# Reordering ten rows of the output projection by column tile, and five weight chunks in place of six, in a one-token attention and MLP kernel

## The chip, the cores and the metric

The kernel runs on one core of one Trainium2 chip. The metric is the device time of one execution in microseconds (us). A ratio is the mean time of one kernel's fast runs over that of the kernel before in the same rounds on the same chip, so it is not quite the ratio of the medians quoted beside it. Verdicts are given at 2%. The profile's span runs from the first to the last instruction and is some 1.3 to 1.7 us shorter than the time.

## The reference, cut to what matters

One token goes through a layer norm, then through attention (32 heads, 4 key/value heads, the last 4096 positions of the cache) and an MLP, and both are added to it:

```python
def reference(A_x, A_k_cache, A_v_cache, A_wq, A_wo, B_x, B_w1, B_b1, B_w2, B_b2):
    # ... q = x @ wq, softmax over 4096 keys, o = p @ v ...
    # attention ends in  o.reshape(B, Sq, Hq * Dh) @ wo      (4096 x 1024)
    # MLP:  h = gelu(y @ w1 + b1);  h @ w2 + b2              (1024 x 3584, 3584 x 1024)
    x = A_x
    xn = _layernorm(x, axis=-1)
    return x + _A_ref(xn, ...) + _B_ref(xn, ...)
```

With one token, every weight is read once and used for one row. About 40 MB have to come in (39.88 MB in the profile), and there is little arithmetic. The last weight in the stream is wo, which TensorE takes as 32 rows of 128 x 1024, each as two matmuls of 512 columns, one for each half of the output.

## The kernel before

All large transfers go through one queue, in program order. wo comes last, in chunks, each with a semaphore of its own:

```python
W2_CHUNKS = [28]
WO_CHUNKS = [15, 9, 4, 2, 1, 1]
WO_IN_W1 = sum(WO_CHUNKS[:2])
# ... the two halves of the output lie in PSUM on partitions 0 and 32: here called two column tiles
    ACC = [PS[32 * n: 32 * n + 1, (6 + n) * 512: (7 + n) * 512] for n in range(2)]
# ...
    for j, nj in enumerate(WO_CHUNKS):
        if j0 == WO_IN_W1:
            sp.wait_ge(PE.sem, pe_sc)
        sp.dma_start(wo_at(j0, nj), wo_pm[:, j0 * D:(j0 + nj) * D]).then_inc(s_wo[j], 16)
        j0 += nj
# ...
    for j, nj in enumerate(WO_CHUNKS[:-1]):
        pe.wait_ge(s_wo[j], 16)
        for _ in range(nj):
            for n in range(2):
                pe.matmul(ACC[n], lhsT=OP[:, r:r + 1], rhs=wo_at(r, 1)[:, n * 512:(n + 1) * 512],
                          start=False, stop=False)
            r += 1
# ... the last row stands in a block of its own, followed by the casts and the output
    with nc.body("pe_last", valid_engines=TENSOR):
        pe.wait_ge(s_wo[-1], 16)
        # ... two matmuls ...
        last.then_inc(s_fin, 1)
```

Just before this loop, 56 matmuls of the same kind work off w2 (L537), and before those 32 matmuls take the values of the attention (L504). "Column tile" means no more here than what the trace of this kernel shows: the two matmuls of a wo or w2 row, into partitions 0 and 32, start 3 to 7 ns apart, while the 32 of L504, all into partitions 0 to 31, start 0.216 us apart at full clock and 0.427 at half.

## Time and profile before

| | before |
|---|---|
| time, median of the first 3 runs | 98.81 us (98.73 to 98.90) |
| span of the profiled run | 97.6 us |
| bytes moved, mean rate | 39.88 MB, 409 GB/s |
| TensorE busy | 67.3 us (69%) |
| mean granted clock | 0.895 |

These are lines of the page's second part: the span in 40 equal slices of 2.44 us, with the busy tenths of TensorE, the granted clock in tenths of full speed, and the busy tenths of the transfers.

```profile
PE   0001299959992039988999982169994799891991
PEclk9999999999999655999999999955699759999579
DMA  7999999989999989979999998889994999899970
```

The transfers are busy almost everywhere. TensorE has holes, and a few slices after some of them the clock dips to half. The last dip lies in the tail, a few slices from the end. The other views (chain, timeline, windows) are shown in the prediction.

### The profile page before, as it was taken

The page shows a single profiled execution, that of the slowest core. Times are in us where ns is not written, and L with a number is a line of the kernel's source. Part 1 is how long each engine was busy: PE and PEld are TensorE (multiplying, and loading weights), DVE is VectorE, ACT ScalarE, POOL GpSimd, SP SyncE. Part 2 cuts the span into 40 slices and gives each one's busy share as a digit, 9 for nine tenths or more (in the row PEclk, how much of TensorE's full clock was granted, in tenths as well). Part 3 has the DMA queues.
Part 4 walks back from the last instruction along what each step waited for, and adds up shares of the span by engine and source line. Part 5 has one row for each costly group of instructions (what it writes and reads, how often), then busy time and mean ns, then how long its engine had stood idle before and what let it go on. Part 6 is the DMA issues. An engine that isn't in the chain of part 4 may idle for free.

```text
span 97.6 us, 1050 instructions
## 1 busy us (share of the span) xinstructions
PE 67.3 (69%) x330; PEld 31.8 (33%) x330; DVE 36.0 (37%) x49; ACT 5.8 (6%) x11; POOL 7.1 (7%) x23
## 2 busy tenths in 40 slices
PE   0001299959992039988999982169994799891991
PEld 0001255525541025645654421033341233330330
DVE  3705530000008999600999515794005300000002
ACT  0500060000001000000000000400000000000002
POOL 6795000000000000000000000000000000000000
PEclk9999999999999655999999999955699759999579
DMA  7999999989999989979999998889994999899970
GB/s 215 430 432 431 431 430 430 430 346 426 490 446 470 399 376 517 423 336 430 430 430 423 423 671 376 376 376 399 634 470 201 428 466 466 383 408 401 413 272 8
DMA packets 2773, 39.88 MB, mean 409 GB/s; under 512 B 322, under 2 KB 340, under 8 KB 724
## 3 DMA queue, kind: packets, MB, share of 16 engines
q1 hardware_dynamic: 2738, 39.85, 96.0%
q8 instruction: 1, 0.02, 0.1%
q10 hardware_dynamic: 34, 0.01, 0.1%
HBM read 39.86 MB, written 0.00 MB: 408 GB/s over the span
## 4 chain that ended last, share of the span: by engine, by line
DMA 82%; PE 13%; SPq 2%; issue 1%; DVE 1%; POOLq 0%
DMA W<-in_B_w_dram 42%; DMA W<-in_A_wo_dram 40%; PE PS L387 7%; PE PS L548 5%; SPq L168 1%; DVE KV L567 1%; SPq L178 0%; SPq L426 0%; SPq L162 0%; PE PS L557 0%; POOLq L260 0%
## 5 line engine op out<-in xcount | busy, mean ns | idle before, releaser
L344 DVE STREAM_TRANSPOSE KV<-KV 128x4096 bf16<-128x4096 bf16 x4 | 17.5, 4424 | 5.7 <-DMA KV<-in_A_k_cache_dram 5.7
L387 PE MATMUL PS<-W,YZ 128*97 x64 | 14.7, 387 | 4.6 <-POOLq L260 4.5
L335 PE MATMUL PS<-WA,PT 128*97 x64 | 15.5, 404 | 1.3 <-POOLq L260 1.2
L387 PEld LDWEIGHTS PS<-W,YZ 128*97 x64 | 8.7, 136 | 10.6 <-issue 7.8
L335 PEld LDWEIGHTS PS<-WA,PT 128*97 x64 | 8.5, 132 | 8.0 <-issue 3.7
L504 PE MATMUL PS<-KV,PT 128*32 128x512 bf16 x32 | 9.7, 479 | 0.1
L548 PE MATMUL PS<-W,OP 128*1 128x512 bf16 x48 | 7.2, 461 | 2.3 <-DMA W<-in_A_wo_dram 2.3
L537 PE MATMUL PS<-WA,GT 128*1 128x512 bf16 x56 | 7.9, 451 | 0.0
L567 DVE CAST KV<-PS 1x512 bf16<-1x512 f32 x1 | 0.7, 683 | 18.8 <-PE PS L557 18.8
L403 PE MATMUL PS<-KV,LQ 128*128 x32 | 7.1, 379 | 0.0
L295 PE MATMUL PS<-XT,meanf 128*128 128x16 f32 x2 | 0.6, 384 | 9.4 <-DVE XT L291 9.4
L347 DVE STREAM_TRANSPOSE TT<-PS 128x1024 f32<-128x1024 f32 x1 | 1.2, 1250 | 15.5 <-PE PS L335 15.5
L504 PEld LDWEIGHTS PS<-KV,PT 128*32 128x32 bf16 x32 | 3.7, 117 | 5.7 <-issue 3.7
L548 PEld LDWEIGHTS PS<-W,OP 128*1 128x1 bf16 x48 | 2.2, 94 | 6.8 <-DMA W<-in_A_wo_dram 2.5
L403 PEld LDWEIGHTS PS<-KV,LQ 128*128 x32 | 3.1, 98 | 3.9 <-issue 0.6
L537 PEld LDWEIGHTS PS<-WA,GT 128*1 128x1 bf16 x56 | 2.7, 96 | 4.7 <-issue 2.3
L295 PEld LDWEIGHTS PS<-XT,meanf 128*128 128x128 f32 x2 | 0.5, 310 | 9.4 <-DVE XT L291 9.4
L509 DVE TENSOR_TENSOR TT<-PS,RM 32x512 f32<-32x512 f32 x1 | 0.7, 678 | 7.0 <-PE PS L504 7.0
L451 ACT ACTIVATE Pe<-PS,NMB 128x512 bf16<-128x512 f32 x2 | 1.3, 683 | 29.1 <-DVE NMB L448 29.1
L205 DVE MEMSET PS<- 128x3072 f32 x1 | 2.6, 2618 | 0.6 <-issue 0.6
L430 DVE TENSOR_REDUCE MXP<-PS 128x1 f32<-128x1024 f32 x1 | 1.2, 1225 | 3.0 <-PE PS L403 3.0
L569 ACT ACTIVATE KV<-PS 1x512 bf16<-1x512 f32 x1 | 0.6, 586 | 29.5 <-PE PS L557 29.5
(87 smaller groups left out, 31.5 us busy)
## 6 DMA issues: line engine op xcount, KB each, us to landing
WA<-in_A_wq_dram SPq DMA_DIRECT2D x2, 4096.0 KB, 16.6
W<-in_B_w_dram SPq DMA_DIRECT2D x2, 3584.0 KB, 37.2
WA<-in_B_w_dram SPq DMA_DIRECT2D x1, 7168.0 KB, 46.2
KV<-in_A_k_cache_dram SPq DMA_DIRECT2D x4, 1024.0 KB, 34.1
KV<-in_A_v_cache_dram SPq DMA_DIRECT2D x4, 1024.0 KB, 43.3
W<-in_A_wo_dram SPq DMA_DIRECT2D x1, 3840.0 KB, 33.5
W<-in_A_wo_dram SPq DMA_DIRECT2D x1, 2304.0 KB, 38.6
KV<-in_A_wo_dram SPq DMA_DIRECT2D x1, 1024.0 KB, 34.4
```

The source lines that it names most:

```text
L205: d_ps = DVE.mark(dve.memset(PS[:, 0:6 * 512], 0.0))
L335: last = pe.matmul(PS[0:97, n * 512:(n + 1) * 512], lhsT=shifted(XZ, s)[:, bass.ds(k, 1), :], rhs=wq_rows[:, bass.ds(k, 1), s * 1024 + n * ...
L344: dve.transpose(out=KT[:, g * W:(g + 1) * W], in_=KT[:, g * W:(g + 1) * W]).then_inc(r_k, 1)
L347: DVE.mark(dve.transpose(out=TT[:, :], in_=PS[:, 0:1024]))
L387: last = pe.matmul(PS[0:97, (2 + n) * 512:(2 + n) * 512 + HW], lhsT=shifted(YZ, s)[:, bass.ds(k, 1), :], rhs=w1_rows[:, bass.ds(k, 1), c: ...
L403: last = pe.matmul(PS[:, (4 + n) * 512:(5 + n) * 512], lhsT=q_blocks[:, bass.ds(g, 1), j, :], rhs=k_blocks[:, bass.ds(g, 1), n, :, j, :], ...
L430: d_mxp = DVE.mark(dve.tensor_reduce(out=MXP[:, 0:1], in_=PS[:, 4 * 512:6 * 512], axis=AX.X, op=ALU.max))
L451: a_exp = ACT.mark(act.activation(out=Pe[:, n * 512:(n + 1) * 512], in_=PS[:, (4 + n) * 512:(5 + n) * 512], func=ACTF.Exp, scale=SCALE, bi ...
L504: last = pe.matmul(PS[0:32, 0:512].rearrange("p (g d) -> p g d", g=HKV), lhsT=PT[:, b * 32:(b + 1) * 32], rhs=Vb[:, b, :, :], start=(b == ...
L537: pe.matmul(ACC[n], lhsT=GT[:, c:c + 1], rhs=W2[:, c * D + n * 512: c * D + (n + 1) * 512], start=False, stop=False)
L548: pe.matmul(ACC[n], lhsT=OP[:, r:r + 1], rhs=wo_at(r, 1)[:, n * 512:(n + 1) * 512], start=False, stop=False)
L567: d_out = DVE.mark(dve.tensor_copy(OUT[32:33, :], ACC[1]))
```

## The change

The intent is to close the hole that TensorE has while it waits for the second wo chunk, without adding an instruction. Matmuls of the two halves normally run side by side on two column tiles (a pair every 0.216 us at full clock in the profile before). If ten rows are issued as ten matmuls of one half and then ten of the other, they should not pair (those of L504, on one tile, take 0.216 us each), TensorE should stay busy longer, and the clock should not fall before the tail. The chunks after the second become 5, 2 and 1 rows.

```diff
-WO_CHUNKS = [15, 9, 4, 2, 1, 1]
+WO_ALONE = 10
+WO_CHUNKS = [15, 9, 5, 2, 1]
...
-        for _ in range(nj):
-            for n in range(2):
-                pe.matmul(ACC[n], lhsT=OP[:, r:r + 1], rhs=wo_at(r, 1)[:, n * 512:(n + 1) * 512],
-                          start=False, stop=False)
-            r += 1
+        alone = WO_ALONE if j == 0 else 0
+        order = [(u, n) for n in range(2) for u in range(alone)] + [(u, n) for u in range(alone, nj) for n in range(2)]
+        for u, n in order:
+            pe.matmul(ACC[n], lhsT=OP[:, r + u:r + u + 1], rhs=wo_at(r + u, 1)[:, n * 512:(n + 1) * 512],
+                      start=False, stop=False)
+        r += nj
```

## The prediction

The change needs only the step of matmuls on one column tile, and the trace gives it: 0.216 us at full clock for L504. That the stream could give no more than its 430 to 432 GB/s is not shown.

> **What bounds the kernel now.** I read the page's chain of waits first, then the chain in order of time for the last 13 us, then the timeline of TensorE there, then the windows cut where the granted clock changes, and last each transfer's issue and landing. The chain by line:
>
> ```profile
> DMA 82%; PE 13%; SPq 2%; issue 1%; DVE 1%; POOLq 0%
> ...
> 51.43 38.63 DMA W<-in_A_wo_dram
> 90.06 0.04 issue
> 90.10 5.30 PE PS L548 x32
> 95.41 0.24 PE PS L557 x2
> 95.64 0.02 issue
> 95.67 0.68 DVE KV L567
> ```
>
> The first line is the share of the span by engine; the rest are start, length and owner. The kernel streams weights through one queue (39.88 MB, mean 409 GB/s over the span, about 430 in most slices), and the chain is that stream until the second wo chunk lands at 90.06 us. From there to the end it is TensorE: 32 matmuls of L548, then the last two. The timeline shows why these take over 5 us (start, length, engine, line, count, idle before):
>
> ```profile
> 76.53 7.89 PE L537 MATMUL PS<-WA,GT 128*1 128x512 bf16 x56
> 84.70 3.40 PE L548 MATMUL PS<-W,OP 128*1 128x512 bf16 x30 [0.28 <-DMA W<-in_A_wo_dram]
> 90.10 3.78 PE L548 MATMUL PS<-W,OP 128*1 128x512 bf16 x18 [2.00 <-DMA W<-in_A_wo_dram]
> 93.66 1.74 PE L548 MATMUL PS<-KV,OP 128*1 128x512 bf16 x14
> 95.24 0.38 PE L557 MATMUL PS<-KV,OP 128*1 128x512 bf16 x2
> ```
>
> 30 matmuls of the first chunk take 3.40 us, then TensorE stands idle 2.00 us, then 18 matmuls of the same form take 3.78 us. The windows (stretch, length, TensorE busy, granted clock, DMA share, GB/s) give the reason:
>
> ```profile
> 73.31:76.72 3.41, 1.28 (x11) 1.00 0.67 288
> 76.72:80.14 3.42, 3.42 (x18) 0.50 1.00 431
> 80.14:83.55 3.41, 3.41 (x34) 1.00 1.00 432
> 83.55:86.97 3.42, 3.14 (x32) 1.00 0.98 420
> 86.97:90.38 3.41, 1.41 (x16) 1.00 0.97 414
> 90.38:93.79 3.41, 3.41 (x20) 0.50 0.98 400
> 93.79:97.21 3.42, 1.83 (x18) 1.00 0.21 76
> ```
>
> The clock changes on a grid of 3.41 us. A cell with 1.28 or 1.41 us of work (37 and 41%) is followed by one at half clock; a full cell brings the full clock back. Another cell, 18.70 to 22.11, with 2.26 us of work (66%) was not followed by a fall. So the 2.00 us hole before the second chunk makes the next 3.41 us run at half clock, and TensorE falls behind the stream exactly in the tail. The individual starts are 0.216 us apart by pairs at full clock (0.427 at half), as the first chunk's line also gives: (3.40 - 0.38) / 14 steps between 15 pairs. The two halves of a row start only 4 ns apart, since they lie on different column tiles.
>
> How late TensorE is at the very end matters most. The last transfer is issued at 59.46 and takes 35.5 us, so it lands at about 95.0:
>
> ```profile
> 59.46 0.43 SPq L426 DMA_DIRECT2D KV<-in_A_wo_dram  x1
> ...
> DMA to landing us min/median/max: 35.5/35.5/35.5
> ...
> 95.05 0.08 PEld L557 LDWEIGHTS PS<-KV,OP 128*1 128x1 bf16 x2 [0.15 <-DMA KV<-in_A_wo_dram]
> ```
>
> TensorE took up the last row's weights at 95.05, just after that landing, and its matmuls began at 95.24, one pair step (0.216) after the previous pair at 95.02. So TensorE had nearly caught up: it is late by 0.1 to 0.2 us, not by the 1.7 us that the half clock cost it in between.
>
> [...]
>
> **The change part by part.** First, the ten rows half by half. The matmul count stays at 64 for wo and the sums are the same up to their order. Ten matmuls in a row on one column tile can't pair, so they take a step of 0.216 us each, then ten on the other. The first of the second tile can start with the tenth of the first, and at the other seam likewise, so the first chunk has 10 + 9 + 5 = 24 steps instead of 15. It starts at 84.70 as before; its last start is 84.70 + 23 x 0.216 = 89.67 and its busy time ends at 89.67 + 0.38 = 90.05. Waste of 9 x 0.216 = 1.94 us, laid exactly into the 2.00 us hole; the second chunk lands at 90.06. L504 shows that a stream on one tile counts as work: after a full cell of it (66.48 to 69.90) the clock came back.
>
> What it buys: the cell 86.97 to 90.38 becomes about 97% busy, so no half clock from 90.38. The nine rows of the second chunk then take 9 x 0.216 = 1.94, from 90.10 to 92.04 (next possible start), where before the tenth row started at 93.66. That is 1.6 us earlier.
>
> Second, the chunks. 4 2 1 1 rows become 5 2 1: same bytes, one transfer fewer, and the last chunk is still one row. Before, the landings are 90.06, then issue plus landing time: 58.14 + 34.4 = 92.5, 93.8, 94.4 and 95.0, that is about 0.615 us a row (256 KB at some 425 GB/s) whatever the chunk size. So five rows land at 90.06 + 5 x 0.615 = 93.14, two more at 94.37, the last at 94.99. [...]
>
> Third, the new tail. TensorE idles from 92.04 (busy to about 92.2) to 93.18, works 5 x 0.216 to 94.26, idles to 94.41, does two rows to 94.84, waits for 94.99 and starts the last pair at about 95.10 (landing to first matmul was 0.13 us for chunk one, 0.04 for chunk two). Before: 95.24. **The end comes 0.14 us earlier**; casts and output stay the same. The cell 90.38 to 93.79 has 1.8 + 0.6 = 2.4 us of work, 71%, over the 66% that kept the clock, so no new half clock there. The sum: 1.6 us gained on TensorE in the middle, 1.5 of them hidden behind the stream. 98.81 - 0.14 = 98.67.
>
> **The rivals.**
> One: the gain at the end equals the gain in the middle (1.6 us, 97.2, 1.6% faster). For it speaks that the chain of waits charges 5.5 us to TensorE after 90.10. Against it: the last chunk's landing at 95.0 doesn't depend on TensorE (no buffer is waited for after 59.46), and nothing can end before it.
> Two: the free phase. If the grid lies otherwise in other executions, the kernel before is not always hit. A cell must hold most of the 2.00 us hole to fall; with cells of 3.41 us I estimate that in 40 to 70% of phases. Where it is not hit, the kernel before also ends at the landing, and the change gives 0.00. Where the half clock starts later than 90.38, the loss before can be some 0.4 us. The small range of the times before (98.73 to 98.90) leaves room for at most about 0.2 us of this. It would make 98.75.
> Three: the waste makes TensorE late. If the half clock falls into the first chunk (a hole before 84.57), eight of its steps take 0.427, and it ends some 1.7 us late, at 91.6; nine, five and two rows then end at 93.5, 94.6 and 95.0, still about at the last landing. If two such things meet, the kernel would be slower by up to 0.5 us: 99.2. Single-tile steps slower than 0.216 would act the same way; 0.2 us of slack at 90.06 and 1.1 at 93.14 absorb 0.05 a step.
> Four: fewer, larger transfers move the last landing itself. Between chunks of 4, 2 and 1 rows the rate hardly differs, so at most some hundredths of a us.
>
> **Range and chances.** The expected gain is 0.14 us in this phase and 0.05 to 0.3 over phases; I keep 98.68. The spread of one kernel is about 0.2 to 0.3 us, larger than the gain. Faster by over 2% needs 96.8, below the landing plus output, which is ruled out unless the stream itself quickens; slower by 2% needs 2 us of new loss, more than the whole hole. So nearly all is within 2%, and the range is 98.45 to 98.95.
>
> **What would show the steps right or wrong.** In the timeline, the first chunk's 30 matmuls should last about 5.35 us (24 steps) and the idle time before the second chunk fall under 0.1 us. The windows after 90 should show clock 1.00, and the second chunk's 18 matmuls about 2.1 us. Waits for wo should appear before chunk three (about 1.0 us), and small ones before four and five, and the chain should end on the transfer, with only the last two matmuls after it. The last landing should stay at 95.0 and the span be 97.4 to 97.5. I'm wrong if the last landing moves by over 0.2 us, if the clock still falls to 0.50 after 90 with a full first chunk (a stream on one tile with one column would then not count as work), or if many executions differ through the phase.

## The result

| | before | after |
|---|---|---|
| time, median of 6 runs | 98.86 us (98.72 to 99.03) | 98.98 us (98.82 to 99.01) |
| ratio | | 1.0008, 95% interval 0.9994 to 1.0022 |
| span of the profiled run | 97.6 us | 97.6 us |
| mean granted clock | 0.895 | 0.913 |

A second measurement in another session (the relabelled run a_again below, with the same instructions) gave 98.72 us against 98.78 for the kernel before, ratio 0.9986 (0.9964 to 1.0008). The two ratios lie on either side of 1. The change moves the time by less than these runs can tell.

The chain of the changed kernel, by engine and then its last pieces in order of time (start, length, owner):

```profile
DMA 70%; PE 25%; SPq 1%; issue 1%; DVE 1%; POOLq 0%
...
58.29 34.94 DMA KV<-in_A_wo_dram
93.23 0.04 issue
93.27 1.24 PE PS L551 x10
...
95.14 0.04 issue
95.18 0.40 PE PS L560 x2
```

The chain now stays with the transfers until the third chunk lands at 93.23, and the last two matmuls start 0.04 us after the last landing (95.14). Before, they started some 0.2 us after theirs. So the end does what the prediction said. But the landing itself is 0.12 us later than in the profile before, and the span is the same. The timeline of TensorE (start, length, line, count, idle before):

```profile
75.99 6.21 PE L538 MATMUL PS<-WA,GT 128*1 128x512 bf16 x56
84.86 8.30 PE L551 MATMUL PS<-W,OP 128*1 128x512 bf16 x48 [2.65 <-DMA W<-in_A_wo_dram]
93.27 1.86 PE L551 MATMUL PS<-KV,OP 128*1 128x512 bf16 x14
```

This is another history than in the profile before. The w2 matmuls took 6.21 us, not 7.89, and the hole lies in front of the first wo chunk, 2.65 us long, not in front of the second. The wait before chunk three, told as about 1.0 us, is 0.11 us (84.86 + 8.30 = 93.16 to 93.27). The windows, cut on the 3.41 us grid on which this execution's clock changed (stretch, length, TensorE busy, clock, DMA share, GB/s):

```profile
72.08:75.49 3.41, 1.59 (x8) 1.00 0.96 413
...
82.31:85.73 3.42, 0.87 (x5) 1.00 0.92 397
85.73:89.15 3.42, 3.42 (x15) 0.50 1.00 431
89.15:92.56 3.41, 3.41 (x31) 1.00 0.97 410
```

The grid lies 2.2 us elsewhere (85.73 against 80.14 + 3.41 = 83.55). The hole at 74 us left 1.59 us of work in its cell this time, where 1.28 had stood before, and w2 ran at full clock. Hence TensorE was done early, the hole before chunk one grew, and the half clock fell into chunk one. The change doesn't alter any instruction before chunk one, and the profiles below show either history with both row orders, so the difference is put down to the phase. The two profiles were of different phases, and a comparison of their tails alone would mislead.

### The profile page after: what moved, and what is told of

Read it like the earlier page. It is cut to its first block, busy times and chain, and to the rows that moved or that the text cites. A ratio compares the mean times of both kernels' runs of the same rounds, so it can differ in the third digit from the quotient of the medians.

```text
span 97.6 us, 1049 instructions
## 1 busy us (share of the span) xinstructions
PE 68.3 (70%) x330; PEld 32.5 (33%) x330; DVE 36.0 (37%) x49; ACT 5.8 (6%) x11; POOL 7.1 (7%) x23
## 4 chain that ended last, share of the span: by engine, by line
DMA 70%; PE 25%; SPq 1%; issue 1%; DVE 1%; POOLq 0%
DMA KV<-in_A_wo_dram 36%; DMA W<-in_B_w_dram 34%; PE PS L388 16%; PE PS L404 7%; PE PS L551 2%; SPq L169 1%; DVE KV L570 1%; PE PS L560 0%; SPq L163 0%; POOLq L261 0%
## 5 line engine op out<-in xcount | busy, mean ns | idle before, releaser
L388 PE MATMUL PS<-W,YZ 128*97 x64 | 15.5, 407 | 3.8 <-POOLq L261 3.8
L336 PE MATMUL PS<-WA,PT 128*97 x64 | 16.5, 423 | 0.3
L551 PE MATMUL PS<-W,OP 128*1 128x512 bf16 x48 | 8.3, 442 | 2.7 <-DMA W<-in_A_wo_dram 2.7
L505 PE MATMUL PS<-KV,PT 128*32 128x512 bf16 x32 | 9.0, 453 | 0.1
L538 PE MATMUL PS<-WA,GT 128*1 128x512 bf16 x56 | 6.2, 379 | 0.0
L551 PEld LDWEIGHTS PS<-W,OP 128*1 128x1 bf16 x48 | 2.9, 91 | 8.0 <-issue 5.4
## 6 DMA issues: line engine op xcount, KB each, us to landing
W<-in_A_wo_dram SPq DMA_DIRECT2D x1, 3840.0 KB, 33.5
W<-in_A_wo_dram SPq DMA_DIRECT2D x1, 2304.0 KB, 38.6
```

The source lines that it names most:

```text
L336: last = pe.matmul(PS[0:97, n * 512:(n + 1) * 512], lhsT=shifted(XZ, s)[:, bass.ds(k, 1), :], rhs=wq_rows[:, bass.ds(k, 1), s * 1024 + n * ...
L388: last = pe.matmul(PS[0:97, (2 + n) * 512:(2 + n) * 512 + HW], lhsT=shifted(YZ, s)[:, bass.ds(k, 1), :], rhs=w1_rows[:, bass.ds(k, 1), c: ...
L505: last = pe.matmul(PS[0:32, 0:512].rearrange("p (g d) -> p g d", g=HKV), lhsT=PT[:, b * 32:(b + 1) * 32], rhs=Vb[:, b, :, :], start=(b == ...
L538: pe.matmul(ACC[n], lhsT=GT[:, c:c + 1], rhs=W2[:, c * D + n * 512: c * D + (n + 1) * 512], start=False, stop=False)
L551: pe.matmul(ACC[n], lhsT=OP[:, r + u:r + u + 1], rhs=wo_at(r + u, 1)[:, n * 512:(n + 1) * 512], start=False, stop=False)
```

## The experiments

For these kernels the two halves of a wo row stand on lines of their own, so that the trace tells them apart; the instructions stay the same. In each of them the matmul of the first half has the lower line number (L552, L555 or the like) and that of the second half is two lines further on.

### Both kernels again, and each part alone

The kernel before, relabelled:

> The kernel before once more, the two halves of wo written on lines of their own, same instructions. A control of the noise and a second look at the clock's phase. Ratio 1.000 within 0.15%. Theory 1 (the clock's 3.41 us grid lies freely against the kernel, and the end is set by the last landing): the half-clock cells lie elsewhere than at 90.38 in this profile with probability of some 70%, or equal ones if the phase is fixed by the launch; the last pair starts 0.05 to 0.6 us after the last landing, depending on it.

The changed kernel, relabelled:

> The changed kernel, halves on lines of their own, same instructions. Time as the changed kernel's, ratio 0.998 to 1.001. Theory F (matmuls start strictly in program order): the first matmul of the second half in chunk one starts with the tenth of the first half, step 9, and the chunk takes 24 steps. Rival W (TensorE starts a matmul on a free column tile ahead of older ones that wait for the other tile, within a window of a few instructions): it starts at step 6 or 7, the chunk takes 21 to 22 steps, and the second half trails to the end of chunk two by about 3 steps. [...] No half-clock cell after 90 in either.

Only the order:

```diff
-WO_CHUNKS = [15, 9, 5, 2, 1]
+WO_CHUNKS = [15, 9, 4, 2, 1, 1]
```

> Ten rows half by half, chunks as before (15 9 4 2 1 1). If the time depends on the last landing alone: ratio 0.998 to 1.001 to the kernel before, equal to the changed kernel; last landing at 4.95 us after the second chunk's; hole before chunk two under 0.2 us. If the half-by-half order brings a gain that the new chunks take back: faster than before by 0.1 to 0.2% while the changed kernel is not.

Only the chunks:

```diff
-WO_ALONE = 10
+WO_ALONE = 0
```

> Chunks 15 9 5 2 1 alone, rows paired as before. If fewer transfers change nothing: last landing 4.95 us after the second chunk's, the 2.0 us hole stays, ratio 0.999 to 1.001. If the larger third chunk costs (work starts 0.6 us later): slower than before by up to 0.3% in executions whose tail runs at half clock, because TensorE starts five rows at 93.2 instead of four at 92.5 and is then behind the landing by more.

| kernel | median us | ratio (95%) | last landing, last pair of its profile |
|---|---|---|---|
| before again | 98.84 | 1.0001 (0.9978 to 1.0024) | 94.81, 94.86 |
| changed again | 98.72 | 0.9986 (0.9964 to 1.0008) | 94.80, 94.84 |
| order alone | 98.76 | 0.9990 (0.9969 to 1.0012) | 94.94, 94.98 |
| chunks alone | 98.78 | 0.9992 (0.9967 to 1.0018) | 94.94, 94.98 |

All four intervals contain 1, and all four last pairs start 0.04 to 0.05 us after the last landing. The kernel before does this too. Its windows in this second profile:

```profile
72.28:75.69 3.41, 1.31 (x7) 1.00 0.96 413
75.69:79.10 3.41, 3.38 (x20) 0.50 1.00 432
...
85.93:89.34 3.41, 1.98 (x20) 1.00 0.96 412
89.34:92.76 3.42, 2.50 (x22) 1.00 1.00 419
```

The same hole of 1.96 us before chunk two is there, but here the grid cuts it in two, its larger part lies with 1.98 us of work, and the clock stays full. So the lateness that the prediction wanted to remove was a property of the phase of that one execution. How often is it so? The profiled execution with half clock in the tail had a mean clock of 0.895. Among the 25 later runs of the kernel before, taken beside the experiments, four have a mean clock of 0.895 and 21 have 0.907 to 0.913. The mean clock doesn't say where the half-clock cells lie, so four of 25 is an estimate of how rare that phase is. It may be too high: one more half-clock cell of 3.41 us lowers the mean by 3.41 x 0.5 / 97.6 = 0.017, which is the step from 0.912 to 0.895, and two later profiles with 0.894 and 0.896 (b_pad, h12_fill) have that cell elsewhere than in the tail. The four took 98.91 us in the mean and the others 98.89. Even there the lateness doesn't stand out, against landings that vary by 0.33 us between these kernels' profiles (94.80 to 95.13).

The order alone shows, in the timeline of its profile at full clock, how chunk one runs (L552 is the first half, L554 the second):

```profile
84.63 1.67 PE L552 MATMUL PS<-W,OP 128*1 128x512 bf16 x7 [0.39 <-DMA W<-in_A_wo_dram]
85.93 0.38 PE L554 MATMUL PS<-W,OP 128*1 128x512 bf16 x1
...
88.30 1.03 PE L554 MATMUL PS<-W,OP 128*1 128x512 bf16 x4
```

The seventh matmul of the first half starts at 84.63 + 1.67 - 0.38 = 85.92, and the first of the second half starts with it, at 85.93, though it stands behind the eighth, ninth and tenth in the program. It overtook three. In the changed kernel again (a_again), where the same chunk ran partly at half clock, it happens with the seventh too, 1.97 us in (84.53 to 86.50) and not 1.30. So in both profiles the count of matmuls passed is three, and the time differs: as theory W told, and not theory F. The last of the second half starts at 88.30 + 1.03 - 0.38 = 88.95, that is 20 steps of 0.216 after the first, so the chunk has 21 steps. It ends at 89.33 and leaves a hole of 0.67 us, where under 0.2 us had been expected for this run.

The chunks alone, with rows in pairs, had the half clock in chunk one, as the changed kernel had. The pairs were done before chunk two landed all the same:

```profile
90.03 0.38 PE L552 MATMUL PS<-W,OP 128*1 128x512 bf16 x1 [0.27 <-DMA W<-in_A_wo_dram]
```

### All fifteen rows half by half

```diff
-WO_ALONE = 10
+WO_ALONE = 15
```

> The changed kernel with all 15 rows of chunk one half by half. Window theory (a matmul on the free column tile passes three older ones that wait for the other): the first matmul of the second half starts together with the 12th of the first, 11 steps in, whatever the clock, and the chunk takes 15 + 15 - 3 = 27 steps, ending at about 90.5 where chunk one runs at full clock, some 0.4 us after chunk two's landing. Strict order would be 29 steps; a window counted in time would start it elsewhere. Time: the slack of 1.1 us before chunk three takes the lateness, ratio 0.998 to 1.002.

The median is 99.11 us (98.64 to 99.21), ratio 1.0003 (0.9971 to 1.0034). The first half's line of the timeline, and the next:

```profile
84.65 4.44 PE L552 MATMUL PS<-W,OP 128*1 128x512 bf16 x12 [2.83 <-DMA W<-in_A_wo_dram]
88.71 0.38 PE L554 MATMUL PS<-W,OP 128*1 128x512 bf16 x1
```

The second half starts with the 12th of the first (84.65 + 4.44 - 0.38 = 88.71), again past three older ones. So the count of three holds here too (the step total that was told, 27, was one too many: the last of the second half starts 25 steps after the first start of the chunk). The ratio lies in the range that was told, but its reason failed in this profile: with half clock in chunk one the last matmul started at 95.40, half a microsecond after the last landing (94.91), so the slack didn't take all of the lateness. The three runs at 0.913 took 99.06 to 99.21, the one at 0.895 took 98.64. The times alone don't tell this kernel from the one before.

### A larger hole, and closing it

Three rows move from chunk one to chunk two, in the kernel before:

```diff
-WO_CHUNKS = [15, 9, 4, 2, 1, 1]
+WO_CHUNKS = [12, 12, 4, 2, 1, 1]
```

> The kernel before with chunks 12 12 4 2 1 1: three rows move from chunk one to chunk two, so the hole before chunk two (landing near 90.0) grows to 3 us or more. Theory 1 (a hole in a 3.41 us cell gives a half-clock cell, and TensorE's lateness shows only where it passes the last landing): nearly every execution has half clock from the cell after 90; of the 20 rows left, eight take 0.427 and twelve 0.216, so the last pair starts near 95.8 to 96.1, 0.8 to 1.1 us after the last landing: 0.6 to 1.0% slower. Rival (the clock in the tail is no matter, the landing sets the end): ratio 1.000.

The same with the change's own means:

```diff
-WO_ALONE = 0
+WO_ALONE = 12
```

> As h12, with all 12 rows of chunk one half by half, the change's own means. Within the window of a few instructions that the first runs showed (the second half starts three rows before the first has ended), the chunk takes 12 + 12 - 3 = 21 steps, not 12: nine steps or 1.9 us of the hole are filled. Theory 1: where the hole of 74 to 76 had given a half-clock cell, chunk one starts late (84.4) and the hole is closed, no half clock after 90; where not, a hole of 2 to 2.6 us stays and half clock comes in some executions. Ratio between those of h12_fill and h12, 0.999 to 1.006. Rival: 1.000.

The larger hole costs: median 100.02 us (99.65 to 100.65), ratio 1.0132 (1.0084 to 1.0179). Its windows:

```profile
86.73:90.14 3.41, 0.27 (x4) 1.00 0.90 384
90.14:93.55 3.41, 3.41 (x18) 0.50 1.00 403
```

A hole of 3.14 us, a cell with 0.27 us of work, half clock after it, and a last pair at 95.78, 0.83 us after the landing (94.95). The expectation of 0.6 to 1.0% was a little low, and the direction and the size of the tail's lateness are as told. (The profile is of the fastest of the four runs; how late the tail is in the others wasn't seen.) With twelve rows half by half the median is 98.89 us (98.78 to 99.03), ratio 0.9993 (0.9972 to 1.0014): all of it is back, and the ranges don't overlap. The mean clocks are 0.912 to 0.930, not 0.878 to 0.897. A line of its timeline and its windows:

```profile
90.32 0.38 PE L552 MATMUL PS<-W,OP 128*1 128x512 bf16 x1 [2.73 <-DMA W<-in_A_wo_dram]
...
85.16:88.57 3.41, 2.43 (x16) 1.00 1.00 432
88.57:91.99 3.42, 1.67 (x16) 1.00 0.87 369
```

The hole was shortened here and not closed. The second half started with the ninth of twelve (84.84), once more past three. Chunk one took 20 steps (83.11 to 87.58; 21 had been told) and not 12, so in pairs it would have ended 8 x 0.216 = 1.7 us sooner, and the hole would have been some 4.5 us (an estimate from these lines; w2 ran at full clock in this execution, unlike in the profile above). What is left of it is 2.73 us, which the grid cut into cells with 2.43 and 1.67 us of work. No half clock came, and the last pair was 0.05 us behind the landing. So the change's idea works where TensorE is late by more than the stream hides. In the kernel before, it isn't.

### Filling the hole with matmuls without use

In the kernel with the larger hole, 16 matmuls into a spare PSUM bank after chunk one:

```diff
+        if j == 0:
+            for u in range(16):
+                pe.matmul(PS[0:1, 0:512], lhsT=OP[:, u % 12:u % 12 + 1], rhs=wo_at(u % 12, 1)[:, 0:512],
+                          start=True, stop=True)
```

> As h12, with 16 matmuls without use (a spare PSUM bank, one column tile, some 3.5 us) after chunk one, in the hole. Theory 1: the hole falls to 1 us or less, no half clock after 90, the twelve rows of chunk two end near 92.6 and the rest waits for landings: last pair 0.05 to 0.2 us after the last landing, ratio 0.998 to 1.002, so 0.6 to 1.0% faster than h12 with 16 matmuls more. Rival: as h12, 1.000, both the same.

This missed: median 99.97 us, ratio 1.0104 (1.0084 to 1.0124). No half clock came after 90, and the last pair was 0.05 us after the landing, as told. But the landing had moved to 96.24. All landings up to w2 (75.39) were as in the other kernels; chunk one came at 84.08 and not at 82.69. Something had held the stream for 1.4 us, and the instruction queue showed two packets and not one. Two runs followed. The first puts 16 matmuls of one column into the kernel before, so that the instructions are added and hardly any work:

```diff
+                pe.matmul(PS[0:1, 0:1], lhsT=OP[:, u % 12:u % 12 + 1], rhs=wo_at(u % 12, 1)[:, 0:1],
+                          start=True, stop=True)
```

> The kernel before with 16 matmuls of one column after chunk one, in the hole: 32 instructions more[...]. Theory I (the slow h12_fill came from its 32 instructions: one more fetch of 16 KB on the instruction queue, which keeps one of the 16 engines for 0.9 us [...]): the instruction queue shows 2 packets, the first near 80, chunk one lands 9.1 + 1.3 us after w2 and not 9.1, the last landing near 96.3, ratio 1.010 to 1.015. Rival (it came from the 3.5 us of TensorE work or from the half clock): landings as before, ratio 0.998 to 1.002.

The second loops over four of the filling matmuls in the kernel with the larger hole:

```diff
+            with nc.Fori(0, 4, 1, engines=TENSOR) as k:
+                for u in range(4):
+                    pe.matmul(PS[0:1, 0:512], lhsT=OP[:, u:u + 1], rhs=wo_at(u, 1)[:, 0:512],
+                              start=True, stop=True)
```

> As h12_fill, the 16 matmuls in a loop of 4 by 4, so about a third of the added instructions. If no further instruction fetch comes (theory I) and theory 1 holds: hole under 1 us, no half clock after 90, last landing near 95.0 and the last pair 0.05 us after it, ratio 0.998 to 1.003, 1% faster than h12. If the loop's branches bring a fetch after all: landings late as in h12_fill, 1.01. If filling the hole doesn't bring the clock back: as h12, 1.008 to 1.018 with half clock after 90.

The padded kernel took 99.91 us, ratio 1.0095 (1.0059 to 1.0131), just under the range of theory I and far from its rival's. Its transfer view, by queue for the whole span, by queue for 79.3 to 79.5 us, and by issue with kilobytes and us to landing:

```profile
q8 instruction: 2, 0.03, 0.1%
...
q8 instruction: 1, 0.02, 28.9%
...
W<-in_A_wo_dram SPq DMA_DIRECT2D x1, 3840.0 KB, 34.8
W<-in_A_wo_dram SPq DMA_DIRECT2D x1, 2304.0 KB, 39.9
```

One packet of 16 KB on the instruction queue took 28.9% of 16 engines over 0.2 us, that is 0.92 us of one engine. After it every landing is 1.2 to 1.3 us later (34.8 and 39.9 us from issue, not 33.5 and 38.6), and the last pair waits for the last landing at 96.18. The time that the one packet takes is less than the delay; what makes up the rest is not settled. The rival, that the filling work or the half clock was to blame, told 0.998 to 1.002 for this kernel and is out. The loop brought such a packet as well, at 80.3: 100.03 us, ratio 1.0116 (1.0078 to 1.0154), last landing 96.15. Its clock stayed full in all cells after 86. The first of them:

```profile
86.76:90.17 3.41, 3.41 (x18) 1.00 0.89 380
```

So with the hole filled the clock stayed full (in the kernel with 16 matmuls too: pairs start 0.21 to 0.22 us apart after 91), but in the three kernels with added instructions the last landing came at 96.15 to 96.24, over 1 us later than without them (94.80 to 95.13). In all three a packet came on the instruction queue in mid-stream; that it is the cause is argued from this, as no run added instructions without one. A filling that only reorders, as the change does, had none: the changed kernel's profile shows one such packet, as the one before does, and it comes after the last landing (96.22 and 96.08 us). Fewer added instructions were not tried.

### Without the stream in front

To see TensorE's own time, one transfer is cut. In the kernel before, chunk three (four rows) is not loaded; in the changed one, four of the five rows of chunk three are not loaded. TensorE works on old data there, so the result is wrong. The comparison with the reference let both pass all the same, which says nothing for them.

```diff
-        sp.dma_start(wo_at(j0, nj), wo_pm[:, j0 * D:(j0 + nj) * D]).then_inc(s_wo[j], 16)
+        a0 = j0 + (4 if j == 2 else 0)
+        if a0 < j0 + nj:
+            sp.dma_start(wo_at(a0, j0 + nj - a0), wo_pm[:, a0 * D:(j0 + nj) * D]).then_inc(s_wo[j], 16)
```

In the cut kernel before, TensorE's wait for that chunk goes too, since nothing is loaded.

> Wrong result on purpose: the kernel before without the transfer of chunk three (four rows of wo; TensorE works on what lies in the buffer), so that the last landing comes 2.46 us earlier, near 92.5, and TensorE, no longer the stream, sets the end. If the stream hid the middle: the last pair starts near 93.5 where the tail runs at full clock (17 rows of 0.216 after 89.9), 1.3 to 1.4 us earlier than before, and near 95.0 where it runs at half clock, hardly earlier; so runs with a mean clock near 0.895 should be about 1.4 us longer than those at 0.91. If the stream hides nothing: all runs 2.4 us faster.

> Wrong result on purpose: the changed kernel without four of the five rows of chunk three in the transfer, the same bytes as in the other cut. Theory (the half-by-half order is real TensorE time, normally hidden by the stream; it pays only in the rarer phase with half clock in the tail): in the common phase, with half clock in chunk one, chunk one trails by 0.65 us into chunk two and the last pair starts near 94.1, so it is some 0.3 to 0.7 us slower than the cut kernel before in executions of the same kind, and about 0.7 to 1.4 us faster than its half-clock ones. Rival (the order saves TensorE time always, as predicted): faster than the cut kernel before by 1 us or more in all.

The cut kernel before took 97.24 us (97.12 to 97.37), the cut changed one 97.42 (97.18 to 97.93); ratios 0.9829 (0.9794 to 0.9865, unclear at 2%) and 0.9838 (0.9801 to 0.9875, the same). The last matmuls in their timelines, first of the cut kernel before, then of the cut changed one:

```profile
93.32 0.38 PE L565 MATMUL PS<-KV,OP 128*1 128x512 bf16 x2
```

```profile
94.12 0.38 PE L564 MATMUL PS<-KV,OP 128*1 128x512 bf16 x1
```

The last landings are at 92.37 and 92.45, so TensorE sets the end here. In the profile with half clock in chunk one the changed order ends 0.8 us later than the order before in a profile with full clock there. The phases differ, so the 0.8 us alone doesn't show the order's share. But the chunks-alone profile above has half clock in chunk one with rows in pairs, and the pairs were still done 0.27 us before chunk two's work began. So what is late here is most likely the added steps; no pair of cut profiles in one phase shows it directly. None of the four runs of the cut kernel before showed the 1.4 us of a half-clock tail; all had a mean clock of 0.911, so that part of the expectation stays untested. The rival, that the new order saves TensorE a microsecond always, is out. The medians differ by only 0.18 us with overlapping ranges, so no more than this is claimed.

## Why the prediction was right or wrong

**Right: the stream sets the end.** The prediction took the last landing as a floor, and in both kernels' second profiles the last pair starts 0.04 or 0.05 us after it. Its rival one (1.6% faster) is ruled out by the result. That the time stays within 2% of the kernel before holds. The first median, 98.98, lies just above the range, the second, 98.72, inside it and near the 98.68 told. That is luck: the kernel before took 98.78 in the same rounds, and by the ratios both are within noise of no change.

**Wrong in size: the gain of 0.14 us.** The failing term is the last line of the third part, the old lag of the last pair. The lag was real in the profile that I had (last pair at 95.24, landing at 95.01), and I carried it into all executions: the profiled one took 99.01 us, and I took the gain from a median of 98.81. In the kernel's second profile the lag is 0.05 us, and 21 of 25 runs have another mean clock. Rival two told of this, but its weight was wrong: I estimated that 40 to 70% of phases would be hit, and the estimate from mean clocks is four of 25. The reason is that the holes are coupled. In the profiles with 15 rows in chunk one where the hole at 74 us didn't bring half clock, w2 ended early (56 matmuls in 6.21 us, not 7.75 to 7.89), a hole of over 2.6 us opened before chunk one (2.65 us in the changed kernel's), and the half clock fell there. Chunk one then ended late, and the hole before chunk two was gone (0.27 us in the profile of the chunks alone). Where w2 did run at half clock, it also mattered how the grid cut the later hole: in the kernel before again it left 1.98 and 2.50 us of work in two cells, and no half clock followed. Of the ten profiles with 15 rows there, six ran w2 at full clock, and all six had the half clock in chunk one; of the other four only the first had it in the tail. I had treated the last hole as if it alone counted. Rival three told of this half clock in chunk one, but the main line took no account of it; it stands in both profiles of the changed kernel. There it uses up the slack: the wait before chunk three, told as about 1.0 us, is 0.1 us in both (93.16 to 93.27, and 92.84 to 92.97).

**Wrong in size: 24 steps for chunk one.** The first part let the second half start with the tenth matmul of the first. It starts with the seventh, and the chunk has 21 steps at full clock: 4.70 us (84.63 to 89.33) and not 5.35, and a hole of 0.67 us, not under 0.1. The part of it that counts still held: in that profile the cell 86.68 to 90.09 (2.74 us of work) was not followed by half clock.

**A reading.** "About 430 in most slices" is true of 15 of the 40 slices (423 to 432); the mean of 409 GB/s is the safer figure.

**Right: the chunks.** Five rows landed 3.06 us after chunk two (90.17 to 93.23), against 3.08 worked out. The last landing stays some 4.95 us after the second's, with six chunks and with five. The chunks alone give 0.9992.

**Right, but only seen elsewhere: hole, half clock, late end.** The kernel before with a hole of 3.14 us shows each link and its price, 1.3%. The reorder takes all of it back by the times; in its profile it shortened the hole and didn't close it. As for the link from hole to half clock: full-clock cells of 3.41 us with 0.27 us of work (larger hole), 0.87 (changed), 1.28 and 1.41 (before) and 1.31 us (before again) were followed by half clock; cells with 1.59 (changed), 1.67 (twelve rows half by half) and 1.98 us (before again) were not, but one with 1.68 us (cut kernel before, 28.29 to 31.71) was. So no edge is claimed. Of the half-clock cells, one with 2.28 us of work (before, 63.07 to 66.48) was followed by another, and those with 3.38 to 3.42 us (before, changed, before again, larger hole) by full clock.

**Where the gain went.** In the common phases there was none to be had, as TensorE already waited for the last landing. In the rare phase about 0.2 us of lag would go (no profile caught the changed kernel in it), which is less than the spread of the landings. And where chunk one runs at half clock the new order spends TensorE time, which the slack before chunk three hides, just. None of the versions above beats both kernels beyond noise; where TensorE isn't late, the end of the span is the last landing plus 2.4 us of last pair, casts and output.

## What to carry to other kernels

Before an idle hole is worked on, look how far after the last landing the last work starts, and look in more than one execution: the clock's grid lay 2.2 us elsewhere in the second of two executions, which makes one profile a sample, and here one hole's phase decided whether the next hole existed (2.00 us in one profile, 0.27 in another). Filling a hole by reordering ten rows of the existing matmuls cost nothing here that the next wait didn't hide (ratios 0.9986 and 1.0008), while added instructions cost more than their work: they came with a packet on the instruction queue in mid-stream and 1% more time (99.91 to 100.03 us). A change that is worth 0.1% in one profile's tail should be tried where the same effect is large (here the larger hole), which tells whether the mechanism exists, apart from whether it pays here.
